# Transposing keys and queries of a head pair in two half-height tiles instead of one full-height tile

## The chip, the cores and the metric

The kernel runs on one core of a Trainium2 chip. A core has TensorE (PE; the loading of its stationary operand is shown apart, as PEld), VectorE (DVE), ScalarE (ACT), GpSimd (POOL) and SyncE (SP, which here issues nearly all DMAs). TensorE writes into PSUM, which has 8 banks of 512 fp32 columns on 128 partitions; VectorE and ScalarE read it from there. The metric is the device time of one execution in microseconds (us), as the median of several runs.

## What is computed

Everything is fp32. First comes attention with random features, for 8 batches of 8 heads, 576 tokens and head width 64; then a Fourier mix of its output with a two-layer network:

```python
def phi(x):                                  # q, k: (8, 8, 576, 64), scaled; omega: (128, 64)
    h = np.einsum('bhsd,md->bhsm', x, omega) - np.sum(x * x, -1, keepdims=True) / 2
    h = h - np.max(h, axis=-1, keepdims=True)
    return np.exp(h) / np.sqrt(m)
kv  = np.einsum('bhsm,bhsd->bhmd', phi(k), v);  z = np.sum(phi(k), axis=2)
x   = einsum('bhsm,bhmd->bhsd', phi(q), kv) / (einsum('bhsm,bhm->bhs', phi(q), z) + 1e-6)
u   = x + real(fft(fft(x, over tokens), over width))      # x as (8, 576, 512)
out = u + relu(normalised(u) @ w_ch1) @ w_ch2             # 512 -> 2048 -> 512
```

The subtraction of the maximum makes the term with the squares fall out, so the kernel computes only the projection, its maximum over the 128 features, and the exponential.

## The kernel before

**Two programs.** The work is written as streams: Python generators that yield a step (which engine or engines may do it, its assumed length, what it waits for, which buffers it takes and gives) and then issue that step's instructions. A planner (class `Listing`, from L100) runs at build time. It always picks the step that can begin first by its own clock, with small preferences (`bias`), and where a step may go to two engines it picks the one that would end first. Instructions go to each engine's queue in the order so picked, and each engine runs its queue in that order. It is a greedy order: nothing is searched, and no order is stored. The planner runs twice. The first program holds the attention, the Fourier mix, the conversion of the weights from another number format, and the preparation of the network; the second holds the network's matrix products.

**A pair.** The attention goes by pairs of heads, 4 per batch, 32 in all (`attn`, L580). Three streams run pairs side by side (`NS = 3`; stream i takes pairs i, i+3, ...). For each pair:

1. `loads` (L376) fetches keys and queries into one tile `kq` of 128 partitions and 18 x 64 columns, by two DMAs on SP's queue: the keys (event `("k", n)`), then the queries (event `("kq", n)`). There are two such tiles.
2. `transposed` (L502) turns the 9 chunks of 128 columns of `kq` into `kqT` by TensorE transposes (a matmul with the identity, L519). A chunk is 128 x 128, one transpose gives 128 columns. They come in groups of 4, 4 and 1; each group is a step, takes one PSUM bank, and is copied to SBUF by `evicted` (L523: ScalarE at L535 or VectorE at L533). The copy gives the bank back.
3. `pairs_of` (L599) projects on the features (matmuls at L613) in three steps of 4, 1 and 4 chunks. In the first six pairs the matmuls use two tiles of 64 rows x 128 columns of the TensorE array ("rows"), later four of 64 x 64 ("quarters"). Each step takes two adjacent PSUM banks ("duo").
4. `softmax` (L549): VectorE takes the maxima (L556), ScalarE the exponentials (L573, into tiles `e`). The exponentials of a bank give that bank back.
5. The products with the values (L647, quarters, a duo), the transposes of the queries' exponentials by the same helper `transposed` (groups of 1, 4 and 4, again at L519, tile `qeT`), and the numerator and denominator (L694 and L702, two tiles of 128 rows x 64 columns, "halves", a duo). VectorE divides (L711, L712, L723).

**Banks.** A step that takes a "bank" gets any one of the 8 that is free first, with a preference for one whose partner is in use. A step that takes a "duo" gets one of the 4 aligned pairs, once both of its banks are free (`banks_at`, L128).

**Tile shapes on TensorE.** Each step has a `mode`: "whole" (the default, and that of transposes), "rows", "halves" or "quarters". The planner adds 0.12 us where the mode changes between neighbouring steps.

The two places that the change rewrites, before:

```python
yield Step(PE, 0.109 * m, after=after(j0, j1), take=("bank",) + ..., give=give(j0, j1), bias=0.14)
...
for j in range(j0, j1):
    nc.tensor.transpose(ps[:, (j - j0) * 128 : (j - j0 + 1) * 128], src(j), ident[:])
yield Fork(evicted(dst, b, j0, j1, makes, order))
...
((0, 4), (4, 8), (8, R)),                      # groups of kqT, R = 9
lambda j0, j1: (("kq", n),) if j1 > 4 else (),  # the first group waits for the keys alone
```

Of the kernel before, what the change touches and what calls it, by code (L numbers as in the profile page):

```python
# [287 lines left out]
def kernel(  # L288
# [10 lines left out]
    nc = tc.nc  # L299

    B, H, S, D = q.shape
# [14 lines left out]
    R = S // 64  # L316
# [30 lines left out]
    ident = const.tile([128, 128], F32, name="ident")  # L347
# [11 lines left out]
        kq=NKQ, turned=NS, e=NE, e1=NS, kv=NS, x0=1, x1=1, fold=1, half=1, y=1,  # L359
# [3 lines left out]
    def psum_of(b):  # L363

        i = b.ids[0]
        return banks[:, i] if len(b.ids) == 1 else banks[:, i : i + 2]

    def got():

        return listing.got, psum_of(listing.got)  # L370
# [131 lines left out]
    def transposed(src, name, groups, after, makes, give, order=None):  # L502


        dst = None
        for j0, j1 in groups:
            m = j1 - j0
            yield Step(
                PE,
                0.109 * m,  # L510
                after=after(j0, j1),
                take=("bank",) + (("turned",) if j0 == 0 else ()),
                give=give(j0, j1), bias=0.14,
            )
            if dst is None:
                dst = att.tile([128, R, 128], F32, name=name, tag="turned")
            b, ps = got()
            for j in range(j0, j1):
                nc.tensor.transpose(ps[:, (j - j0) * 128 : (j - j0 + 1) * 128], src(j), ident[:])  # L519
            yield Fork(evicted(dst, b, j0, j1, makes, order))  # L520
        return dst

    def evicted(dst, b, j0, j1, makes, order):  # L523
        cost = (0.13 + 0.1 * (j1 - j0)) if order else 0.05 + 0.107 * (j1 - j0)
        step = Step(
            {ACT: cost, DVE: 0.06 + 0.133 * (j1 - j0) + (0.06 if order else 0.0)}, late=0.02,
            makes=makes + (j0,), give=(b,), bias=0.08,
        )
        yield step

        def copy(out, in_):
            if step.eng == DVE:
                nc.vector.tensor_copy(out=out, in_=in_)  # L533
            else:
                nc.scalar.activation(out=out, in_=in_, func=AF.Copy)  # L535

        ps = psum_of(b)[:, 0 : 128 * (j1 - j0)].rearrange("q (c p) -> q c p", p=128)
        dst = dst[:, j0:j1, :]
        if order is None:
            copy(dst, ps)  # L540
            return
        h, s, t = order[j0]
        dst = dst.rearrange("q c p -> q (c p)").rearrange("q (h s t c) -> q s h t c", h=h, s=s, t=t)
        ps = ps.rearrange("q c (h t s) -> q s h t c", h=h, s=s)
        for i in range(s):
            of = ps[:, i, :, ::-1, ::-1] if i and j0 else ps[:, i]
            copy(dst[:, i], of)
# [32 lines left out]
    def attn(n):  # L580
        b, pr = divmod(n, NP)

        yield Step(NONE, after=(("k", n),) + ((("vd", n - 1),) if n else ()))
        kq = kqs.pop(n)

        flat = kq[:].rearrange("p c d -> p (c d)")
        kqT = yield from transposed(
            lambda j: flat[:, 128 * j : 128 * j + 128],
            "kqT",
            ((0, 4), (4, 8), (8, R)),  # L590
            lambda j0, j1: (("kq", n),) if j1 > 4 else (),
            ("kqT", n),
            lambda j0, j1: ("kq",) if j1 == R else (),
        )
# [35 lines left out]
        def feature(c):  # L630
# [7 lines left out]
            mode="quarters",  # L638
            after=tuple(("e", n, t) for t in range(3)) + (("vd", n),),
            take=("duo",),  # L640
            give=("e", "e", f"vd{n % NV}"), bias=-0.19,
        )
        kvb, kvp = got()
        for r in range(R):
            for i, h in ((0, 0), (1, 1), (0, 1), (1, 0)):
                rows, cols = slice(D * i, D * i + D), slice(D * h, D * h + D)
# [9 lines left out]
        def keep():  # L656
# [8 lines left out]

        yield Fork(keep())
        qeT = yield from transposed(
            lambda j: feature(R + ORDER_R[j]),
            "qeT",
            ((0, 1), (1, 5), (5, R)),  # L670
            lambda j0, j1: tuple(
                ("e", n, t) for t in sorted({place(R + ORDER_R[j])[0] for j in range(j0, j1)})
            ),
# [7 lines left out]
            mode="halves",  # L681
            after=(("kv", n), ("qeT", n, 0), ("qeT", n, 1), ("qeT", n, 5)),
            take=("duo",),
            give=("turned", "kv"), bias=0.12,
# [28 lines left out]
        dst = x[:, :, 2 * D * pr : 2 * D * (pr + 1)].rearrange("p c (i d) -> p i c d", i=2)  # L713
# [281 lines left out]
    turned = {}  # L995
# [421 lines left out]
    def pairs(start):  # L1417
        for n in range(start, B * NP, NS):
            yield from attn(n)
# [770 lines left out]
```

## Time and profile before

| what | us |
|---|---|
| median of 3 runs (1218.25 to 1226.66) | 1223.65 |
| the profiled execution, its time | 1219.09 |
| its span, first to last instruction | 1217.3 |
| the first kq transpose starts | 4.4 |
| the last kq transpose starts | 356.6 |
| DVE busy in the first 92 us | 76.39 |
| PE busy in the 60 us from 380 to 440 us | 46.22 |
| PE busy in the 100 us from 440 to 540 us | 94.82 |

A profile is one execution taken by the hardware profiler. In a row such as `L519 PE MATMUL banks<-ident,kq 128*128 128x128 f32 x288 | 44.8, 296 | ...`, the parts are the line of the kernel, the engine, the operation, output and inputs, the stationary tile (rows*columns of the array), the moving operand (partitions x columns), the count, and then busy microseconds, mean nanoseconds of one, and the idle time of the engine just before, with what ended it. A matmul of fp32 is two instructions, a transpose is one. Matmuls overlap in the pipeline, so the length of one is its latency; what a matmul costs in a row of them is the distance from start to start. A busy share is an average over its window, and a wait counts only where it delays what ends last.

### The profile page before, as it was taken

The page shows a single profiled execution, that of the slowest core. Times are in us where ns is not written, and L with a number is a line of the kernel's source. Part 1 is how long each engine was busy: PE and PEld are TensorE (multiplying, and loading weights), DVE is VectorE, ACT ScalarE, POOL GpSimd, SP SyncE. Part 2 cuts the span into 40 slices and gives each one's busy share as a digit, 9 for nine tenths or more (in the row PEclk, how much of TensorE's full clock was granted, in tenths as well). Part 3 has the DMA queues.
Part 4 walks back from the last instruction along what each step waited for, and adds up shares of the span by engine and source line. Part 5 has one row for each costly group of instructions (what it writes and reads, how often), then busy time and mean ns, then how long its engine had stood idle before and what let it go on. Part 6 is the DMA issues. An engine that isn't in the chain of part 4 may idle for free.

```text
span 1217.3 us, 32303 instructions
## 1 busy us (share of the span) xinstructions
PE 1121.6 (92%) x12571; PEld 1034.9 (85%) x12571; DVE 974.1 (80%) x1788; ACT 582.1 (48%) x1795; POOL 276.5 (23%) x292
## 2 busy tenths in 40 slices
PE   8888987987579698999998999999999999999998
PEld 7776876876467588999998988999988999988998
DVE  6998999997878767777877687888867799757895
ACT  7867967967484183261253256322355222332221
POOL 2231332321010120032054125500036400044000
PEclk9998998998798799999999899999999999999999
DMA  9745845848743599898879877875776865757453
GB/s 250 228 143 152 246 119 173 244 136 267 235 162 101 155 312 288 259 288 276 271 224 272 280 245 204 263 202 157 236 210 202 262 183 176 211 150 225 134 156 110
DMA packets 209656, 255.83 MB, mean 210 GB/s; under 512 B 55264, under 2 KB 125152, under 8 KB 209504
## 3 DMA queue, kind: packets, MB, share of 16 engines
q1 hardware_dynamic: 209008, 253.50, 68.4%
q8 instruction: 100, 1.64, 0.6%
q14 instruction: 52, 0.43, 0.1%
q10 hardware_dynamic: 496, 0.26, 0.1%
HBM read 200.74 MB, written 57.15 MB: 212 GB/s over the span
## 4 chain that ended last, share of the span: by engine, by line
PE 76%; DVE 9%; ACT 8%; DMA 5%; issue 1%; SPq 0%; POOL 0%; DVEq 0%; ACTq 0%
PE banks L1954 31%; PE banks L1501 26%; ACT e L573 5%; PE banks L1658 4%; PE banks L613 4%; PE banks L647 3%; PE banks L519 3%; PE banks L694 2%; PE banks L806 2%; DVE nmx L556 2%; DMA wl<-w2l 2%; PE banks L816 1%; DMA raw<-in_moe_w_ch_dram 1%; DVE x L933 1%; ACT qeT L535 1%
## 5 line engine op out<-in xcount | busy, mean ns | idle before, releaser
L1954 PE MATMUL banks<-wl,sums 128*128 128x128 f32 x2016 | 250.4, 278 | 0.7 <-DMA wl<-w2l 0.5
L1954 PEld LDWEIGHTS banks<-wl,sums 128*128 128x128 f32 x2016 | 240.4, 195 | 1.6 <-issue 1.0
L573 ACT ACTIVATE e<-banks,nmx 128x128 f32<-128x128 f32 x576 | 159.3, 443 | 32.7 <-DVE nmx L556 32.7
L1954 PE MATMUL banks<-wl,hid 128*128 128x128 f32 x936 | 122.0, 278 | 8.7 <-DMA wl<-w2l 8.3
L1954 PEld LDWEIGHTS banks<-wl,hid 128*128 128x128 f32 x936 | 113.8, 194 | 9.9 <-issue 4.7
L613 PE MATMUL banks<-om,kqT 64*64 64x128 f32 (+1 forms) x2088 | 91.0, 295 | 29.9 <-ACT e L573 23.7
L613 PEld LDWEIGHTS banks<-om,kqT 64*64 64x64 f32 (+1 forms) x2088 | 75.7, 151 | 41.6 <-ACT e L573 29.3
L556 DVE TENSOR_REDUCE nmx<-banks 128x8 f32<-128x1024 f32 (+1 forms) x96 | 87.3, 951 | 20.4 <-PE banks L613 12.9
L1925 ACT ACTIVATE s<-banks 128x128 f32<-128x128 f32 x126 | 34.9, 277 | 132.9 <-PE banks L1954 116.4
L1501 PE MATMUL banks<-unw,wxw 128*128 128x256 f32 x352 | 85.5, 379 | 0.0
L1954 PE MATMUL banks<-wl,hx 128*128 128x128 f32 x576 | 74.3, 275 | 0.4 <-DVE part L1930 0.4
L1501 PEld LDWEIGHTS banks<-unw,wxw 128*128 128x128 f32 x352 | 66.5, 190 | 8.8
L1930 DVE TENSOR_TENSOR part<-banks,s 128x128 f32<-128x128 f32 x114 | 33.0, 290 | 49.6 <-PE banks L1954 44.4
L1501 PE MATMUL banks<-rx,wxw 128*128 128x256 f32 x288 | 71.1, 379 | 0.0
L1526 ACT ACTIVATE s<-banks 128x512 f32<-128x512 f32 x72 | 42.6, 595 | 57.9 <-PE banks L1501 52.2
L1501 PE MATMUL banks<-ttw,wxw 128*128 128x256 f32 x288 | 70.0, 379 | 0.0
L1954 PEld LDWEIGHTS banks<-wl,hx 128*128 128x128 f32 x576 | 69.4, 192 | 0.7 <-DVE part L1930 0.6
L462 POOL TENSOR_TENSOR w<-w,raw 128x512 f32<-128x512 f32 x30 | 41.4, 1379 | 124.9 <-DVE raw L456 110.3
L1501 PEld LDWEIGHTS banks<-rx,wxw 128*128 128x128 f32 x288 | 54.5, 190 | 7.3
L1501 PEld LDWEIGHTS banks<-ttw,wxw 128*128 128x128 f32 x288 | 54.5, 190 | 7.3
L519 PE MATMUL banks<-ident,kq 128*128 128x128 f32 x288 | 44.8, 296 | 17.0 <-ACT e L573 10.9
L1970 ACT ACTIVATE banks<-banks 128x128 f32<-128x128 f32 x63 | 16.6, 263 | 86.3 <-PE banks L1954 83.9
(244 smaller groups left out, 2398.0 us busy)
## 6 DMA issues: line engine op xcount, KB each, us to landing
wl<-w2l SPq DMA_DIRECT2D x294, 256.0 KB, 3.6
wxw<-w1x SPq DMA_DIRECT2D x120, 256.0 KB, 3.2
raw<-in_moe_w_ch_dram SPq DMA_DIRECT2D x32, 512.0 KB, 5.2
kq<-in_k_dram SPq DMA_DIRECT2D x32, 288.0 KB, 4.0
kq<-in_q_dram SPq DMA_DIRECT2D x32, 288.0 KB, 4.2
vd<-in_v_dram SPq DMA_DIRECT2D x32, 288.0 KB, 4.6
wx<-w1x SPq DMA_DIRECT2D x36, 256.0 KB, 3.3
u<-us SPq DMA_DIRECT2D x128, 64.0 KB, 3.1
```

Of the source, the lines that this page charges most:

```text
L462: eng.tensor_tensor(out=dst, in0=dst, in1=lof, op=ALU.add)
L519: nc.tensor.transpose(ps[:, (j - j0) * 128 : (j - j0 + 1) * 128], src(j), ident[:])
L556: nc.vector.tensor_reduce(nmx[:, :, 0:num], pps[:, :, 0 : MF * num].rearrange("p b (c m) -> p b c m", m=MF), axis=AX.X, op=ALU.max, negate ...
L573: nc.scalar.activation(out=e[:, c + (i if num == 1 else 0), :], in_=pps[:, i, MF * c : MF * c + MF], func=AF.Exp, bias=nmx[:, i, c : c + 1],)
L613: nc.tensor.matmul(pps[cols, c, MF * m : MF * m + MF], lhsT=kqT[rows, j, cols], rhs=om2[rows, :],)
L647: nc.tensor.matmul(kvp[cols, i, 0 : D + 1], lhsT=feature(r)[rows, cols], rhs=vds[n % NV][rows, r, :], start=(r == 0), stop=(r == R - 1),)
L1501: nc.tensor.matmul(ps[:, span * f : span * f + span].rearrange("f (b q) -> f b q", q=Q), lhsT=left[:, P * f : P * f + P], rhs=right, start ...
L1526: nc.scalar.activation(out=s[:], in_=ps, func=AF.Copy)
L1658: nc.tensor.matmul(cell.rearrange("f t (b q) -> f t b q", q=Q), lhsT=w[:, d, col : col + 128], rhs=right[:, :, d].rearrange("f (t b) q -> ...
L1925: nc.scalar.activation(out=s[:], in_=ps[:, 0:128], func=AF.Copy)
L1930: nc.vector.tensor_tensor(out=part[:, t, 128 * m : 128 * m + 128], in0=ps[:, 0:128], in1=saved[with_][:], op=ALU.add,)
L1954: nc.tensor.matmul(ps[:, 0:128], lhsT=left[:, f], rhs=wls[head(j), i, n][:, f], start=start and f == 0, stop=(f == 3), skip_group_check=True,)
```

## The change

The first 8 of a pair's 9 key and query transposes become one step. It takes a duo instead of two single banks, waits for keys and queries, and issues two transposes per chunk: rows 0 to 63 of the chunk into the duo's first bank, rows 64 to 127 into its second, 64 columns each, in two tiles of 64 rows ("rows"). The step's assumed length is 0.07 us per chunk instead of 0.109. The two copies of 4 chunks each follow one after the other in one stream; each reads 64 columns per chunk from both banks, and the second one gives both banks back. The ninth chunk stays a whole transpose into a single bank. The transposes of the exponentials (`qeT`) keep their groups and their form. The order is again the planner's greedy one, made anew from the changed steps.

```diff
-        for j0, j1 in groups:
+        for parts in groups:
+            j0, j1 = parts[0][0], parts[-1][1]
             m = j1 - j0
+            split = len(parts) > 1
             yield Step(
                 PE,
-                0.109 * m,
+                (0.07 if split else 0.109) * m,
+                mode="rows" if split else "whole",
                 after=after(j0, j1),
-                take=("bank",) + (("turned",) if j0 == 0 else ()),
+                take=("duo" if split else "bank",) + (("turned",) if j0 == 0 else ()),
                 give=give(j0, j1), bias=0.14,
             )
...
             for j in range(j0, j1):
+                if split:
+                    for r in range(2):
+                        rows = slice(D * r, D * r + D)
+                        nc.tensor.transpose(
+                            ps[:, r, (j - j0) * D : (j - j0 + 1) * D], src(j)[rows, :], ident[rows, rows]
+                        )
+                    continue
                 nc.tensor.transpose(ps[:, (j - j0) * 128 : (j - j0 + 1) * 128], src(j), ident[:])
-            yield Fork(evicted(dst, b, j0, j1, makes, order))
+            yield Fork(evicted(dst, b, parts, makes, order))
...
-    def evicted(dst, b, j0, j1, makes, order):
+    def evicted(dst, b, parts, makes, order):
+        for j0, j1 in parts:
+            yield from copied(dst, b, j0, j1, parts, makes, order)
+
+    def copied(dst, b, j0, j1, parts, makes, order):
+        split = len(parts) > 1
...
-            makes=makes + (j0,), give=(b,), bias=0.08,
+            makes=makes + (j0,), give=(b,) if j1 == parts[-1][1] else (), bias=0.08,
...
+        dst = dst[:, j0:j1, :]
+        if split:
+            k0 = D * (j0 - parts[0][0])
+            ps = psum_of(b)[:, :, k0 : k0 + D * (j1 - j0)].rearrange("q r (c p) -> q c r p", p=D)
+            copy(dst.rearrange("q c (r p) -> q c r p", r=2), ps)
+            return
...
-            ((0, 4), (4, 8), (8, R)),
-            lambda j0, j1: (("kq", n),) if j1 > 4 else (),
+            (((0, 4), (4, 8)), ((8, R),)),
+            lambda j0, j1: (("kq", n),),
...
-            ((0, 1), (1, 5), (5, R)),
+            (((0, 1),), ((1, 5),), ((5, R),)),
```

More of the change, by code (lines that the diff above doesn't have):

```diff
@@ L535, in copy @@
                 nc.scalar.activation(out=out, in_=in_, func=AF.Copy)
+        dst = dst[:, j0:j1, :]
[4 more added lines that the diff above has]
+            return
         ps = psum_of(b)[:, 0 : 128 * (j1 - j0)].rearrange("q (c p) -> q c p", p=128)
-        dst = dst[:, j0:j1, :]
         if order is None:
```

## The prediction

> **What bounds it now.** I read the page first (busy times, then the chain that ended last), then the busy time by stretches, then the order of TensorE's work around the transposes, then the rows of the tiles kq and kqT and the waits. From the page:
>
> ```profile
> PE 1121.6 (92%) x12571; PEld 1034.9 (85%) x12571; DVE 974.1 (80%) x1788; ACT 582.1 (48%) x1795; POOL 276.5 (23%) x292
> ...
> L519 PE MATMUL banks<-ident,kq 128*128 128x128 f32 x288 | 44.8, 296 | 17.0 <-ACT e L573 10.9
> ```
>
> TensorE at 92% is an average over two programs. The transposes of keys and queries (288 = 32 pairs x 9) all lie in the first of them: the last starts at 356.6 us. The busy times by stretches split it (columns: window, length, then PE, PEld, DVE, ACT, POOL with instruction counts, granted clock, DMA share, GB/s):
>
> ```profile
> 92.00:184.00 92.00, 77.99 (x1760) 66.95 (x1760) 84.98 (x163) 72.34 (x272) 27.97 (x21) 0.93 0.60 175
> 184.00:276.00 92.00, 77.34 (x1760) 66.62 (x1760) 86.06 (x167) 73.72 (x283) 25.58 (x21) 0.94 0.62 184
> 276.00:380.00 104.00, 79.90 (x1654) 68.36 (x1654) 79.48 (x158) 69.17 (x259) 12.93 (x12) 0.87 0.63 207
> ...
> 540.00:1217.00 677.00, 667.24 (x4837) 635.31 (x4835) 527.14 (x930) 229.33 (x573) 157.05 (x175) 0.99 0.70 213
> ```
>
> From 540 us on TensorE is the bound (99%), and the change does not touch that work. In the attention stage VectorE is the fullest: 85 to 86 us of 92 (93%), TensorE 84 to 85%, ScalarE 79 to 80%. The same 1,760 matmuls come back in each 92 us: the order repeats every 8 pairs. So TensorE time saved here is worth only what it takes out of waits.
>
> **The step itself.** TensorE's order, first where projections in row tiles stand beside kq transposes, then around another pair (start, length, work, count):
>
> ```profile
> 27.48 1.28 PE L647 MATMUL banks<-vd,e 64*64 64x65 f32 x72
> ...
> 31.94 0.40 PE L702 MATMUL banks<-kv,qeT 128*64 128x65 f32 x8
> 32.27 2.28 PE L613 MATMUL banks<-om,kqT 64*128 64x128 f32 x36
> 34.48 1.09 PE L519 MATMUL banks<-ident,kq 128*128 128x128 f32 x8
> ```
>
> ```profile
> 136.55 1.28 PE L647 MATMUL banks<-vd,e 64*64 64x65 f32 x72
> 137.76 0.33 PE L519 MATMUL banks<-ident,e 128*128 128x128 f32 x1
> 137.93 1.15 PE L519 MATMUL banks<-ident,kq 128*128 128x128 f32 x9
> ...
> 140.28 2.20 PE L613 MATMUL banks<-om,kqT 64*64 64x128 f32 x72
> 142.40 1.15 PE L694 MATMUL banks<-kv,qeT 128*64 128x65 f32 x32
> ```
>
> A group's length is its count of steps plus one matmul's latency (0.27 us for 128 columns, 0.23 for 65). Removed: whole transposes cost (1.15-0.27)/8 = 0.110 us each, so 8 cost 0.88. Added: 16 half-height ones, 8 rounds of two row tiles with 64 moving columns. No row has that shape. The nearest by moving length are the 65-column rounds: quarters (1.28-0.23)/71 x 4 = 0.059 us, halves (1.15-0.23)/31 x 2 = 0.059. The nearest by tile (64x128, two row tiles) is (2.28-0.27)/35 x 2 = 0.115, but with 128 columns moving. So a round costs 0.059 to 0.115. I take 0.059, because the moving length sets the step in all three. The other candidate is the weight load, still 128 columns wide:
>
> ```profile
> L613 PEld LDWEIGHTS banks<-om,kqT 64*128 64x128 f32 x216 | 13.5, 188 | 2.0 <-ACT kqT L535 0.9 <-ACT e L573 0.5 <-issue 0.2
> L519 PEld LDWEIGHTS banks<-ident,kq 128*128 128x128 f32 x288 | 34.7, 150 | 23.1 <-ACT e L573 14.6 <-DVE x L723 5.7 <-ACT kqT L535 0.9
> ...
> L694 PEld LDWEIGHTS banks<-kv,qeT 128*64 128x64 f32 x1024 | 34.2, 140 | 10.8 <-DVE bmp L925 4.3 <-issue 2.0 <-ACT qeT L535 2.0
> ```
>
> A transpose's load (150 ns, mean) is nearer to a 64-column load (140), which keeps a 0.059 round, than to a 128-column load of a matmul (188). I lean on that. The Trainium skill, "TensorE: Matmul & The Clock Gate", section on LDWEIGHTS, says otherwise: a load's time goes by its columns, about columns/1.2 ns, whatever the rows, so halving the height saves nothing; for 128 columns that is an estimate of 107 ns per round, and the saving below would be 0.8 us in place of 13.1. The load rows by line contradict it for transposes as far as a length can.
>
> Saved: 8 x (0.110-0.059) = 0.41 us per pair, 13.1 us over 32 pairs (by the upper end a loss of 8 x 0.005 x 32 = 1.3).
>
> **Changes of tile shape.** Between groups of different tile shape a gap shows: the last of the eight L702 starts at 31.94+0.40-0.23 = 32.11, the next group at 32.27, 0.16 us later where a round takes 0.06: 0.10 us. After L613 it is 142.40-(140.28+2.20-0.27) = 0.19 against 0.09 to the next round: 0.10 again. Eight half-height ones, then the ninth whole: one change more where quarters or halves stand on both sides, two more where a whole transpose went before (as at 137.76), none between row-tile projections (34.48, in the first six pairs). Taken as 1.5 x 32 x 0.10 = 4.8 us, ends 0 and 6.4. Net TensorE time: 13.1-4.8 = 8.3 us saved, 0.26 per pair.
>
> **What of it reaches the end.** In 92 to 276 us VectorE's idle time before its maxima (L556) that a projection (L613) ended is 5.5 us in 6 waits. A kq step 0.26 us shorter shortens each by at most that: 6 x 0.26 = 1.6 us in 184 us, 3.3 over the 380 us of the stage. The rest of the 8.3 us becomes TensorE idle time behind VectorE. Taken: -3.3, ends 0 and -13.1.
>
> **Evictions.** 64 copies of 512 columns (ScalarE 655 ns each) stay; each now reads both banks in runs of 64. The row of that kind, ScalarE's copy into y (L829: 256 columns over two banks in runs of 64), takes 429 ns; between the 362 of 128 columns and the 655 of 512, a straight line gives 460. So no surcharge (ends -30 and +30 ns, 2 us of ScalarE time either way, beside its 20% idle). But both banks are held until the second copy is done, and the first copy is placed only after all 8 transposes.
>
> **The wait for two banks.** The step now asks for an adjacent pair. In the repeating order TensorE has one long wait, at the kq transposes, for exponentials that free banks:
>
> ```profile
> 185.58 2.28 ACT L573 ACTIVATE e<-banks,nmx 128x128 f32<-128x128 f32 x8 [4.39 <-DVE nmx L556]
> 186.78 0.66 PE L519 MATMUL banks<-ident,kq 128*128 128x128 f32 x4 [4.07 <-ACT e L573]
> 187.73 0.62 ACT L535 ACTIVATE kqT<-banks 128x512 f32<-128x512 f32 x1
> 187.91 1.33 PE L519 MATMUL banks<-ident,kq 128*128 128x128 f32 x5 [0.48 <-ACT e L573]
> 188.21 1.17 ACT L573 ACTIVATE e<-banks,nmx 128x128 f32<-128x128 f32 x4
> ```
>
> The first four start on one bank at 186.78, the rest on the next at 187.91. Needing both, all wait until 187.91, with the projections (L613) queued behind them, and the first copy (0.62 us at 187.73) moves behind. I charge that copy, 0.65 us, once per period, 4 periods: +2.6 us.
>
> **The load.** The first step now waits for the queries too, the second DMA of the pair, issued 0.4 us after the keys on SP's queue. Later pairs' loads are issued some 6 us before use (180.05, used 186.78) and land in 4.2: covered. If that lead is gone, 0.6 us per pair. The first pair is exposed: +0.5 us once.
>
> **Sum.** -3.3+2.6+0.5 = -0.2 us: 1218.9 against the profiled execution's 1219.09 (span 1217.3 and 1.8 around it). That execution lies 4.6 us under the median 1223.65, so in the median's terms 1223.4, rounded to 1223.
>
> **Rivals.** (1) Slower by bank waits: each time a transpose waits for exponentials (12.5 us, 11 times in the first 460 us), the second bank comes one set of four exponentials later (1.17 us at 188.21), and the projections behind do not catch up: 11 x 1.17 = 12.9, 1236. It decides from about three such waits on, where it eats the 3.3. For: the waits are there at single banks; against: at 190.63 the projection waited for the later copy anyway. Also the Trainium skill's "TensorEngine Tiling (Array Packing)", section on restrictions, warns that row tiling raises pressure on PSUM banks; the rows above show the banks already short.
> (2) The loads set the round, or the halves run in turn, so that the change does not do what it says: no saving, 4.8+1.3 us of extra TensorE time of which a third to all arrives, plus 3.1: +5 to +9, 1229 to 1233. For: the row-tile row at 0.115; against: the short transpose load.
> (3) Faster: TensorE is most of the chain of waits also in this stage, and all of 8.3 to 13.1 lands: 1210 to 1215. Against: VectorE at 93%.
> (4) The list order falls into another cycle: the 4.3 us hole per period goes or comes twice, 4 times: 1206 or 1241.
>
> **Chances.** Forecast (1217 to 1230) 0.48; (1) 0.20; (2) 0.10; (3) 0.14; (4) 0.08, half each way. A measurement tells 1% (12.2 us) from no change. Slower by more: half of (1), half of (4), and tails of the forecast and (2), 0.06: 0.20. Faster: a third of (3), half of (4) and 0.02 of tail: 0.11. Within: 0.69. The range takes in (3), (2), (1) and the near part of (4): 1208 to 1239.
>
> **What would show it.** In the changed profile: 512 half-height transposes (64x64 moving) at 0.059 us a round, against 0.115 for (2); gaps of 0.10 at more shape changes; the period still near 92 us with VectorE at 93%; idle time before L519 by exponentials about as now, and near 24 us in all for (1). The prediction is wrong if the period changes by over 3 us, or if VectorE's share drops while TensorE's idle time grows.

## The result and the profile after

The changed kernel takes 1233.34 us (median of 6 runs, 1229.96 to 1236.46), the kernel before, run beside it, 1221.56 (6 runs, 1218.25 to 1226.66). The ratio is 1.0091, with a 95% interval of 1.0071 to 1.0110: slower by 0.9% (11 us by the ratio, 12 by the medians), where no change was forecast. The profiled execution spans 1228.2 us, against 1217.3.

First the busy times of the changed kernel's page, then its busy times by stretches, with the windows and columns of before:

```profile
PE 1120.8 (91%) x12827; PEld 1035.4 (84%) x12827; DVE 972.0 (79%) x1777; ACT 574.9 (47%) x1752; POOL 279.4 (23%) x310
```

```profile
92.00:184.00 92.00, 75.25 (x1779) 66.15 (x1768) 82.92 (x154) 69.61 (x254) 30.07 (x25) 0.89 0.61 182
184.00:276.00 92.00, 75.22 (x1775) 65.17 (x1775) 84.24 (x158) 68.23 (x256) 26.14 (x24) 0.93 0.66 194
276.00:380.00 104.00, 79.76 (x1699) 67.88 (x1699) 83.37 (x161) 66.96 (x249) 15.66 (x20) 0.87 0.59 196
380.00:440.00 60.00, 42.68 (x357) 33.79 (x356) 36.06 (x80) 12.87 (x47) 8.12 (x7) 0.72 0.34 105
...
540.00:1217.00 677.00, 670.12 (x4866) 638.68 (x4866) 530.91 (x933) 234.07 (x583) 162.94 (x184) 0.99 0.71 214
```

The stretch from 380 to 440 us of the kernel before:

```profile
380.00:440.00 60.00, 46.22 (x253) 38.01 (x252) 45.38 (x95) 20.18 (x56) 9.11 (x11) 0.86 0.58 189
```

From 540 us on TensorE is as full as before (99%). From 92 to 276 us TensorE, VectorE and ScalarE are all emptier: VectorE has 82.92 and 84.24 of 92 us (84.98 and 86.06 before), TensorE 75 (77 to 78 before). The emptiest stretch is 380 to 440 us, where VectorE had 45.38 us of work before and has 36.06 now, at a granted clock of 0.72 (before 0.86).

Next, the rows of the changed step, by shape, up to 400 us:

```profile
L525 PE MATMUL banks<-ident,kq 64*128 64x64 f32 x512 | 25.2, 242 | 7.7 <-ACT e L593 5.8 <-DVE bmp L933 0.9 <-DVE x L743 0.5
L525 PEld LDWEIGHTS banks<-ident,kq 64*128 64x128 f32 x512 | 21.0, 150 | 11.9 <-ACT e L593 6.4 <-issue 2.0 <-DVE x L743 1.2
...
L550 ACT ACTIVATE kqT<-banks 128x512 f32<-128x512 f32 x63 | 35.2, 613 | 25.8 <-PE banks L525 25.7
L529 PE MATMUL banks<-ident,kq 128*128 128x128 f32 x32 | 9.4, 329 | 3.5 <-DVE x L743 2.6 <-ACT e L593 1.0
```

TensorE's idle time before these transposes has fallen, from 17.0 to 7.7+3.5 = 11.2 us. ScalarE's idle time before the copies into kqT, waiting for the transposes, has risen to 25.8. The same row of before, by shape:

```profile
L535 ACT ACTIVATE kqT<-banks 128x512 f32<-128x512 f32 x57 | 33.9, 655 | 4.2 <-PE banks L519 3.9
```

The two waits of over 4 us for exponentials before kq transposes that the kernel before has in its repeating part, at 94.4 and 186.8 us, are gone. But TensorE now waits about as long in other places. From the waits of the changed kernel (what waited, for what, us in all, times, longest):

```profile
PE banks L633 <- DVE bmp L945: 8.1, 2, 4.1
PE banks L1119 <- ACT e L593: 5.1, 2, 4.7
```

These are projections (L633) that wait for the Fourier mix on VectorE, and transposes of the network's preparation (L1119) that wait for exponentials.

**Where the 11 us appear.** The last steps of the first program, from the timelines of the two traces:

| step | before | after | later by |
|---|---|---|---|
| the last pair's kq transposes start | 355.1 | 365.7 | 10.6 |
| the last maximum starts | 366.5 | 373.3 | 6.8 |
| the last division starts | 378.7 | 401.6 | 22.9 |
| the last folds of the Fourier mix start | 395.4 | 410.3 | 14.9 |
| the first sum after the mix that waits for a DMA (rx) starts | 415.1 | 428.7 | 13.6 |
| the first product of the second program (wl) starts | 448.0 | 460.8 | 12.8 |
| from there to the end of the span | 769.3 | 767.4 | -1.9 |

So in these two executions all of it lies ahead of the second program. In the changed kernel's order of TensorE's work, one line stands out (start, length, work, count, idle time before and what ended it):

```profile
357.78 0.71 PE L525 MATMUL banks<-ident,kq 64*128 64x64 f32 x16
358.42 0.33 PE L529 MATMUL banks<-ident,kq 128*128 128x128 f32 x1
...
375.72 3.62 PE L1678 MATMUL banks<-unT,w 128*128 128x256 f32 x16
...
385.84 8.90 PE L1678 MATMUL banks<-unT,w 128*128 128x256 f32 x40
...
395.58 1.15 PE L714 MATMUL banks<-kv,qeT 128*64 128x65 f32 x32
...
399.90 1.31 PE L714 MATMUL banks<-kv,qeT 128*64 128x65 f32 x30 [0.22 <-ACT qeT L550]
...
406.60 2.50 PE L826 MATMUL banks<-cs_sb,fold 128*128 128x160 f32 x8 [5.16 <-DVE fold L799]
```

The network's first products (L1678) run before the last two pairs' numerators (L714), which VectorE and then the last batch's mix (L826) wait for. In the kernel before the same three kinds of work stand the other way round:

```profile
375.53 1.65 PE L694 MATMUL banks<-kv,qeT 128*64 128x65 f32 x32
377.25 1.10 PE L694 MATMUL banks<-kv,qeT 128*64 128x65 f32 x32
...
382.44 3.72 PE L1658 MATMUL banks<-unT,w 128*128 128x256 f32 x16
```

### The profile page after: what moved, and what is told of

Its sections match the earlier page's. It is cut to its first block, busy times and chain, and to the rows that moved or that the text cites. A ratio compares the mean times of both kernels' runs of the same rounds, so it can differ in the third digit from the quotient of the medians.

```text
span 1228.2 us, 32758 instructions
## 1 busy us (share of the span) xinstructions
PE 1120.8 (91%) x12827; PEld 1035.4 (84%) x12827; DVE 972.0 (79%) x1777; ACT 574.9 (47%) x1752; POOL 279.4 (23%) x310
## 4 chain that ended last, share of the span: by engine, by line
PE 61%; DMA 2%; DVE 2%; ACT 0%; SPq 0%; issue 0%; POOL 0%; DVEq 0%
PE banks L1974 31%; PE banks L1521 27%; PE banks L1678 2%; DMA wl<-w2l 2%; DMA w1x<-rx 0%; DVE ttw L1318 0%; DVE so L1477 0%; DVE w1s L1424 0%; DMA wxw<-w1x 0%; DVE unxw L1215 0%; DVE rx L1477 0%; DMA us<-x 0%; SPq L967 0%; DVE unw L1215 0%; DVE hid L1564 0%
## 5 line engine op out<-in xcount | busy, mean ns | idle before, releaser
L633 PE MATMUL banks<-om,kqT 64*64 64x128 f32 (+1 forms) x2088 | 96.5, 308 | 36.8 <-ACT e L593 22.7
L633 PEld LDWEIGHTS banks<-om,kqT 64*64 64x64 f32 (+1 forms) x2088 | 81.8, 161 | 47.3 <-ACT e L593 26.9
L667 PE MATMUL banks<-vd,e 64*64 64x65 f32 x2304 | 52.1, 245 | 4.8 <-ACT kqT L550 1.9
```

The costliest lines, as they stand in the source:

```text
L633: nc.tensor.matmul(pps[cols, c, MF * m : MF * m + MF], lhsT=kqT[rows, j, cols], rhs=om2[rows, :],)
L667: nc.tensor.matmul(kvp[cols, i, 0 : D + 1], lhsT=feature(r)[rows, cols], rhs=vds[n % NV][rows, r, :], start=(r == 0), stop=(r == R - 1),)
```

## The experiments

The change does several things at once: another form of transposes, a common pair of banks, a common wait, and through the planner another order of the whole first program. The planner sees a step's assumed length, its mode, its buffers and its waits, but not the instructions it issues. So an order can be kept while the instructions are exchanged, and the other way round. Four explanations were tried: the new order alone, with its tail part (the products ahead of the last numerators); the new form; the clock of TensorE, which a shorter step may let fall; and the first copy, which now waits for more. Ratios below are to the kernel before, run beside each; where two changed kernels are compared, their ratios are, because the kernel before had slightly different medians (1221.56 to 1223.80).

### The form at a fixed order

e1: the changed kernel's order, but whole transposes, four in each bank, and copies that read one bank.

```diff
                 if split:
-                    for r in range(2):
-                        rows = slice(D * r, D * r + D)
-                        nc.tensor.transpose(
-                            ps[:, r, (j - j0) * D : (j - j0 + 1) * D], src(j)[rows, :], ident[rows, rows]
-                        )
+                    r, c = divmod(j - j0, 4)
+                    nc.tensor.transpose(ps[:, r, 128 * c : 128 * c + 128], src(j), ident[:])
                     continue
...
-            k0 = D * (j0 - parts[0][0])
-            ps = psum_of(b)[:, :, k0 : k0 + D * (j1 - j0)].rearrange("q r (c p) -> q c r p", p=D)
-            copy(dst.rearrange("q c (r p) -> q c r p", r=2), ps)
+            ps = psum_of(b)[:, (j0 - parts[0][0]) // 4].rearrange("q (c p) -> q c p", p=128)
+            copy(dst, ps)
```

> The changed kernel with its order kept instruction for instruction (the planner is given the same numbers), but the 8 transposes of the pair of banks are whole ones, 4 in each bank, and each copy reads its own bank. Theory ORDER (the half-height transposes do save TensorE time; the loss comes from the order that the greedy planner makes out of the new step): at the same order the whole ones cost 8 x (0.110-0.061) = 0.39 us per pair and save about 0.1 us of shape change, 9 us of TensorE time in all, of which a quarter to all arrives: 1235.5 to 1242 against 1233.3 of the changed kernel. Theory TILE (the half-height form itself costs the time, by shape changes and waits): equal or faster than the changed kernel, down to the 1221.6 of before.

Measured: 1228.04, ratio 1.0035 (1.0011 to 1.0059). The half-height form at this order gives 1.0091: it costs 0.56%, and the intervals don't meet. That is 6.8 us by the ratios, 5.3 by the medians. The changed order with the old form is still slower than before, by 0.35% or 4.3 us. The rows of e1 that stand against those of the changed kernel above:

```profile
L547 ACT ACTIVATE kqT<-banks 128x512 f32<-128x512 f32 x63 | 36.2, 618 | 23.1 <-PE banks L524 21.2 <-DVE rden L727 0.6 <-DVE x L739 0.6
```

With the old form, too, ScalarE is idle for 23.1 us before these copies (25.8 in the changed kernel, 4.2 before). So nearly all of that wait came with the order. The two profiled executions took 1229.51 (e1) and 1229.96 us, closer together than the medians: in them the first wl product starts 5.7 us later with the half-height form, but the time from there to the end is 5.2 us shorter. So the loss at the end is a matter of the medians, not of these two traces.

e2: the kernel before with the common step and the common wait alone. Transposes whole, the planner told 0.109 us per chunk and the mode "whole". So it has an order of its own.

```diff
-                take=("bank",) + (("turned",) if j0 == 0 else ()),
+                take=("duo" if split else "bank",) + (("turned",) if j0 == 0 else ()),
...
-            ((0, 4), (4, 8), (8, R)),
-            lambda j0, j1: (("kq", n),) if j1 > 4 else (),
+            (((0, 4), (4, 8)), ((8, R),)),
+            lambda j0, j1: (("kq", n),),
```

> The kernel before with one part of the change: the 8 transposes stay whole, but are one step with a pair of banks, held until the second copy, waiting for keys and queries; the planner is given their true cost (0.109 us each, mode whole). Theory BANK (asking for two banks at once costs the time): slower than before by most of the 11.8 us, 1229 or more, with more TensorE idle time ahead of the kq transposes than the 17.0 us of before. Theory ORDER: nothing systematic; a new order, somewhere within 10 us of 1221.6 on either side.

Measured: 1217.57, ratio 0.9960 (0.9937 to 0.9983). Two banks at once and one wait for both loads cost nothing in an order that the planner makes for them.

e3: e2's order, with the half-height transposes and copies of the change put in (the first edit, turned round).

```diff
-                    r, c = divmod(j - j0, 4)
-                    nc.tensor.transpose(ps[:, r, 128 * c : 128 * c + 128], src(j), ident[:])
+                    for r in range(2):
+                        rows = slice(D * r, D * r + D)
+                        nc.tensor.transpose(
+                            ps[:, r, (j - j0) * D : (j - j0 + 1) * D], src(j)[rows, :], ident[rows, rows]
+                        )
...
```

> The same order as e2 (the planner is given 0.109 us and mode whole), but the 8 transposes are issued half-height, 64 rows to a bank. Theory ORDER: faster than e2 by a quarter to all of 8 us of TensorE time, 2 to 8 us. Theory TILE: equal to e2 or slower.

Measured: 1220.42, ratio 0.9980 (0.9960 to 1.0001), against e2's 0.9960: no gain again, and a loss of 0.2% that the overlapping intervals don't settle.

### The tail of the order

e4: the changed kernel, its first products held until the last two pairs are divided.

```diff
     def first_products():
-        yield Step(NONE, after=("w2 done",))
+        yield Step(NONE, after=("w2 done", ("x", B - 1, NP - 2), ("x", B - 1, NP - 1)))
```

> The changed kernel, but the first products of the network (L1678 there), which in it stand ahead of the last two pairs' numerators on TensorE from 375.7 us on, wait for the last two pairs' outputs. Theory ORDER, tail part: the last pair's division comes near 380 instead of 401.8 us, and of the 11.8 us of loss 5 to 10 go: 1223 to 1228. Rival: the products only move behind and are waited for there, so that the time stays at 1231 to 1236, and the loss lies in the steady part (a period of 95 instead of 92 us).

Measured: 1230.08, ratio 1.0060 (1.0040 to 1.0080). The same stretch of TensorE's order in e4:

```profile
385.89 1.31 PE L714 MATMUL banks<-kv,qeT 128*64 128x65 f32 x30 [0.22 <-ACT qeT L550]
...
390.39 14.08 PE L1678 MATMUL banks<-unT,w 128*128 128x256 f32 x64
...
410.87 2.50 PE L826 MATMUL banks<-cs_sb,fold 128*128 128x160 f32 x8 [5.49 <-DVE fold L799]
```

The last division starts at 387.5, 14 us earlier than after the change. But now the products (14.08 us) stand ahead of the mix, which starts at 410.87 and not at 406.60; the first wl product starts at 460.7, as after the change at 460.8. So the striking line of the timeline is worth 0.3% of the 0.9% at most (the intervals overlap), and nothing by this trace. The order paid for it in the next place.

### The clock and the first copy

At one place of the same order, e1 and the changed kernel part by 2.6 us. TensorE's order in e1, then in the changed kernel:

```profile
187.71 1.09 PE L524 MATMUL banks<-ident,kq 128*128 128x128 f32 x8 [1.47 <-ACT e L589]
...
190.20 1.28 PE L663 MATMUL banks<-vd,e 64*64 64x65 f32 x72 [1.29 <-ACT kqT L547]
191.30 2.15 PE L629 MATMUL banks<-om,kqT 64*64 64x128 f32 x72
193.38 1.09 PE L524 MATMUL banks<-ident,kq 128*128 128x128 f32 x8
```

```profile
189.10 0.96 PE L525 MATMUL banks<-ident,kq 64*128 64x64 f32 x16 [1.47 <-ACT e L593]
...
191.59 2.23 PE L667 MATMUL banks<-vd,e 64*64 64x65 f32 x72 [1.26 <-ACT kqT L550]
193.59 3.89 PE L633 MATMUL banks<-om,kqT 64*64 64x128 f32 x72
197.41 0.71 PE L525 MATMUL banks<-ident,kq 64*128 64x64 f32 x16
```

The same 144 matmuls take 3.2 us in e1 (190.20 to 193.38) and 5.8 in the changed kernel (191.59 to 197.41). The busy times of the changed kernel in stretches of 3.4 us show TensorE at half its clock there (the columns as above; the last but two is the granted clock):

```profile
183.50:186.90 3.40, 3.40 (x82) 2.99 (x85) 3.26 (x8) 2.20 (x9) 2.15 (x4) 1.00 0.62 212
186.90:190.30 3.40, 1.93 (x43) 1.33 (x35) 3.40 (x4) 2.65 (x10) 3.40 (x5) 1.00 0.59 155
190.30:193.70 3.40, 2.14 (x77) 2.12 (x80) 3.37 (x12) 2.70 (x9) 1.38 (x3) 0.51 0.85 246
193.70:197.10 3.40, 3.40 (x73) 3.40 (x72) 3.13 (x6) 1.31 (x5) 0.30 (x1) 0.50 0.74 205
```

After a stretch in which TensorE was busy for 1.93 of 3.40 us the granted clock is 0.5 for two stretches. In e1 the same place has the same busy time, and the clock stays up:

```profile
185.50:188.90 3.40, 1.94 (x35) 1.47 (x27) 3.40 (x4) 2.64 (x10) 3.40 (x5) 1.00 0.65 168
188.90:192.30 3.40, 2.11 (x112) 2.10 (x115) 3.37 (x12) 3.35 (x13) 1.38 (x3) 1.00 0.88 262
```

So the busy time alone doesn't tell when the clock falls; the last section has an estimate that does better. The other difference is the first copy into kqT. One pair in the changed kernel, then one in e1:

```profile
197.41 0.71 PE L525 MATMUL banks<-ident,kq 64*128 64x64 f32 x16
198.16 1.08 ACT L550 ACTIVATE kqT<-banks 128x512 f32<-128x512 f32 x2 [2.97 <-PE banks L525]
```

```profile
193.38 1.09 PE L524 MATMUL banks<-ident,kq 128*128 128x128 f32 x8
194.07 1.08 ACT L547 ACTIVATE kqT<-banks 128x512 f32<-128x512 f32 x2 [1.21 <-PE banks L524]
```

The sixteen half-height transposes take 0.71 us, the eight whole ones 1.09. But the copy starts 0.75 us after the first half-height transpose and 0.69 after the first whole one: it reads both banks, so it waits for all sixteen; a copy of one bank needs only the first four. Over all 32 pairs of the two traces, taken pair by pair, the first copy comes later after its first transpose by 0.06 us in the median and 0.15 in the mean. In both timelines above TensorE's next work waited for such a copy (the lines that an ACT kqT ended). Four runs tried to part the clock from the copy.

e5: the changed kernel, each half-height transpose issued twice, so that TensorE works longer and a clock that fell for want of work would stay up.

```diff
-                    for r in range(2):
+                    for r in (0, 1) * 2:
```

> The changed kernel, its order kept, but each of the 16 half-height transposes is issued twice into the same place (32 in all), 0.49 us more TensorE time per pair, 15.6 us over 32 pairs. Theory CLOCK (the shorter step leaves more stretches of 3.4 us in which TensorE is busy less than 0.4 of the time; after such a stretch its clock is granted at half, and the half-speed stretches cost more than the step saved): with the time put back there are fewer half-speed stretches, near e1's 79 us in the first 430 us instead of the changed kernel's 102, and the time falls to e1's, 1226 to 1230, although TensorE does more. Rival TILE (the half-height form costs by its shape changes, which are here unchanged): no gain, and the added work makes it slower by a quarter to all of 15.6 us: 1237 to 1249.

Measured: 1241.74, ratio 1.0142 (1.0115 to 1.0168), 0.51% or 6.2 us above the changed kernel. Eight rounds of 0.065 us (worked out below) in 32 pairs are 16.6 us of added TensorE time, so about a third arrives. The half-speed time ahead of the second program went from 102 us to 92 only (e1: 79), each in one profiled execution; the expectation's 102 and 79 are these, while the first 430 us alone have 93 and 75, and 73 in this run. Over whole spans, the mean granted clock of the six runs is 0.953 to 0.961, against 0.949 to 0.955 in the changed kernel and 0.957 to 0.967 in e1's runs. So the clock did rise, and the time did not fall. But the added work also delays the first copy, so this run alone doesn't decide.

e6: e2 with each whole transpose issued twice.

```diff
-                    nc.tensor.transpose(ps[:, r, 128 * c : 128 * c + 128], src(j), ident[:])
+                    for _ in range(2):
+                        nc.tensor.transpose(ps[:, r, 128 * c : 128 * c + 128], src(j), ident[:])
```

> e2 (whole transposes, a pair of banks, its own order) with each of the 8 whole transposes issued twice, 0.88 us more TensorE time per pair, 28 us over 32 pairs. Theory CLOCK says that work in this place can pay for itself where it lifts a stretch over 0.4, but e2 already has few half-speed stretches (72 us in the first 430): between e2's 1217.6 less 4 and plus 8, fewer half-speed stretches than e2. Rival TILE: slower than e2 by a quarter to all of 28 us, 1225 to 1245.

Measured: 1240.38, ratio 1.0131 (1.0103 to 1.0159), against e2's 0.9960: +1.71% or 20.9 us, for 8 x 0.110 x 32 = 28.2 us of added work ahead of the copies. So time in this step is far from free: three quarters of it arrive. That suggests, without showing it, that a saving which brought the copies forward would count.

e9: e1 with chunk j in bank j mod 2, so that the first copy must wait for all eight whole transposes; the work of TensorE and the order are e1's.

```diff
-                    r, c = divmod(j - j0, 4)
+                    c, r = divmod(j - j0, 2)
                     nc.tensor.transpose(ps[:, r, 128 * c : 128 * c + 128], src(j), ident[:])
...
-            ps = psum_of(b)[:, (j0 - parts[0][0]) // 4].rearrange("q (c p) -> q c p", p=128)
-            copy(dst, ps)
+            c0 = (j0 - parts[0][0]) // 2
+            ps = psum_of(b)[:, :, 128 * c0 : 128 * c0 + 256].rearrange("q r (c p) -> q c r p", p=128)
+            copy(dst.rearrange("q (c r) p -> q c r p", r=2), ps)
```

> e1 (the changed kernel's order, 8 whole transposes), but chunk j goes to bank j modulo 2 of the pair, so that the first copy reads both banks and must wait for all 8 transposes, as the changed kernel's first copy must for all 16. TensorE's work and the order are those of e1; only the first copy starts later, by about 0.4 us where ScalarE waits for it. Theory COPY (what the pair waits for is the first copy, which in e1 starts 0.69 us after the first transpose and in the changed kernel 0.75: the half-height step saves nothing there): slower than e1, 3 to 12 us, 1231 to 1240. Rival: TensorE's time is what counts, and the time stays at e1's, 1226 to 1230.

Measured: 1232.06, ratio 1.0077 (1.0044 to 1.0110), 0.42% above e1's 1.0035. The intervals overlap (up to 1.0059 and from 1.0044), so it supports a cost of the later first copy without proving its size. And this copy is much later than the changed kernel's: by 0.44 us in the median pair against e1 (mean 0.45), where the half-height form makes 0.06 (mean 0.15). In proportion to the measured 0.42%, an estimate, the later copy would account for 0.06% to 0.14% of the 0.56% that the half-height form loses to e1, about a quarter at most. The rest would need another cause.

e10: the changed kernel, the ninth transpose issued four times. This adds work behind the common step and leaves the first copies alone.

```diff
-                nc.tensor.transpose(ps[:, (j - j0) * 128 : (j - j0 + 1) * 128], src(j), ident[:])
+                for _ in range(4 if name == "kqT" else 1):
+                    nc.tensor.transpose(ps[:, (j - j0) * 128 : (j - j0 + 1) * 128], src(j), ident[:])
```

> The changed kernel, its order kept, with the ninth transpose, which is whole and stands behind the 16 half-height ones in a bank of its own, issued four times: 0.33 us of TensorE time per pair, about what the half-height form saved, put back behind the two copies that the projections wait for. Theory CLOCK: fewer half-speed stretches, and the time falls towards e1's, 1226 to 1230. Rival (clock of no weight, TensorE's time counts in part): slower by a quarter to all of 10.5 us, 1236 to 1244.

Measured: 1235.66, ratio 1.0106 (1.0064 to 1.0147): 0.15% above the changed kernel, within the intervals. So 3 x 0.110 x 32 = 10.6 us of TensorE time behind the copies cost little or nothing, but they don't win back what e1 has over the changed kernel either. The mean clock of the first 430 us is the last column but two (the changed kernel, e1, e10):

```profile
0.00:430.00 430.00, 342.77 (x7179) 294.66 (x7179) 349.77 (x672) 287.95 (x1048) 104.82 (x106) 0.89 0.59 178
```

```profile
0.00:430.00 430.00, 344.37 (x6926) 296.09 (x6927) 355.24 (x682) 289.29 (x1048) 105.08 (x106) 0.91 0.60 182
```

```profile
0.00:430.00 430.00, 351.84 (x7273) 302.92 (x7274) 347.83 (x669) 289.45 (x1047) 104.56 (x106) 0.90 0.58 176
```

These are single executions. Over the whole span of every run the clock of e10 is 0.954 to 0.962 (mean 0.959), the changed kernel's 0.949 to 0.955 (mean 0.953). So in e5 and e10 the added work brought the clock part of the way back, and in neither did the time fall to e1's 1226 to 1230, as the clock theory had forecast. That the added 10.6 us of e10 cost so little may be the clock's doing. Two things are seen: half-speed stretches lie where e1 and the changed kernel part, and the clocks of their runs (0.957 to 0.967 and 0.949 to 0.955) don't overlap. That the lower clock is the cause of the loss isn't shown: in the rows above the clock fell after a stretch with waits, so it may be a consequence of them.

### The order

An order here includes the choice of engine, where the planner has one. TensorE's instructions are the same in the changed kernel, e8 and e11 (12,827); of the other engines' steps a few change place (ScalarE has 1,752, 1,751 and 1,765).

e7: the kernel before with one line of the diff, so that the first group waits for the queries too. No instruction is edited.

```diff
             ((0, 4), (4, 8), (8, R)),
-            lambda j0, j1: (("kq", n),) if j1 > 4 else (),
+            lambda j0, j1: (("kq", n),),
```

> The kernel before with one line of the change: the first group of transposes waits for the queries too, not for the keys alone. Groups of 4, 4 and 1 whole transposes in single banks as before. Theory ORDER: the wait itself is covered (loads lead by some 6 us), but the planner makes another order of it, and the time lands anywhere within 15 us of 1221.6, on either side. Rival WAIT (the later start is what costs): slower by 2 to 10 us.

Measured: 1206.87, ratio 0.9864 (0.9840 to 0.9889). A wait added, and the kernel is 1.4% faster.

e8: the changed kernel's instructions; the planner is told the mode "whole" for the common step, and so doesn't charge the change of shape.

```diff
                 (0.07 if split else 0.109) * m,
-                mode="rows" if split else "whole",
+                mode="whole" if split else "whole",
```

> The changed kernel with the same instructions, but the planner is told that the half-height step needs no change of tile shape (mode whole instead of rows, 0.07 us each kept). Nothing but the order differs. Theory ORDER: the time moves by 3 to 15 us from 1233.3 on either side, more likely down, since the changed kernel's order has the last two pairs behind the network's products. Theory TILE: the time stays within 3 us of 1233.3, since every cost of the step is still there.

Measured: 1217.07, ratio 0.9939 (0.9920 to 0.9959), 1.5% faster than the changed kernel, with the same work in another order.

e11: as e8, and the planner is told 0.075 us per chunk in place of 0.07. Of some 70 such changes of the planner's numbers, this is the one whose order ends soonest by its own clock.

```diff
-                (0.07 if split else 0.109) * m,
-                mode="rows" if split else "whole",
+                (0.075 if split else 0.109) * m,
+                mode="whole" if split else "whole",
```

> The changed kernel with the same instructions, but the planner is given 0.075 us per chunk instead of 0.07 and mode whole instead of rows; of some 70 such small changes of numbers this order closes soonest by the planner's own clock. Theory ORDER: as fast as e7, 1200 to 1212, so that the spread over orders of the same instructions is over 20 us. Rival TILE: not below 1217.

Measured: 1203.33, ratio 0.9849 (0.9810 to 0.9888), the fastest version found, 30 us under the changed kernel.

e12: e11's order with e1's whole transposes and copies.

```diff
-                    for r in range(2):
-                        rows = slice(D * r, D * r + D)
-                        nc.tensor.transpose(
-                            ps[:, r, (j - j0) * D : (j - j0 + 1) * D], src(j)[rows, :], ident[rows, rows]
-                        )
+                    r, c = divmod(j - j0, 4)
+                    nc.tensor.transpose(ps[:, r, 128 * c : 128 * c + 128], src(j), ident[:])
...
```

> The order of e11, kept, with 8 whole transposes in place of the 16 half-height ones, 4 in each bank. The third comparison of the two forms at one order, after e1 against the changed kernel (whole faster by 0.56%) and e2 against e3 (whole faster by 0.2%). Theory COPY: equal or faster than e11, by 0 to 7 us. If half-height is worth its TensorE time: slower than e11 by 3 to 9 us.

Measured: 1203.95, ratio 0.9856 (0.9815 to 0.9897). At the best order, too, the form makes no difference that can be told.

The first products with wl, in the rows of the changed kernel, e7 and e11 (count, shortest, median and longest in ns, first and last start in us):

```profile
L1974 PE MATMUL banks<-wl,hid x936: 272/275/423, 460.8 to 1214.6; 128*128 128x128 f32 x188
```

```profile
L1954 PE MATMUL banks<-wl,hid x936: 272/275/426, 432.6 to 1189.8; 128*128 128x128 f32 x188
```

```profile
L1974 PE MATMUL banks<-wl,hid x936: 272/275/426, 432.7 to 1188.4; 128*128 128x128 f32 x188
```

The second program starts 28 us earlier in e7 and e11. And the stretch from 380 to 440 us of e11, to be held against the row shown for the changed kernel:

```profile
380.00:440.00 60.00, 56.68 (x277) 48.19 (x278) 41.91 (x79) 29.03 (x64) 9.79 (x12) 0.89 0.70 237
```

TensorE is busy 56.68 of 60 us there, against 42.68: the network's preparation is already running. All orders side by side, ordered by time (from the timelines; the order of instructions is the same within a block):

| kernel | last pair's kq transposes | last division | first wl product | median | ratio |
|---|---|---|---|---|---|
| e11 half-height | 347.2 | 363.2 | 432.7 | 1203.33 | 0.985 |
| e12 whole | 346.7 | 362.8 | 433.6 | 1203.95 | 0.986 |
| | | | | | |
| e7 | 351.9 | 365.9 | 432.6 | 1206.87 | 0.986 |
| | | | | | |
| e8 half-height | 356.4 | 375.1 | 447.4 | 1217.07 | 0.994 |
| | | | | | |
| e2 whole | 355.9 | 378.6 | 446.1 | 1217.57 | 0.996 |
| e3 half-height | 359.1 | 381.7 | 448.5 | 1220.42 | 0.998 |
| | | | | | |
| before | 355.1 | 378.7 | 448.0 | 1221.56 | 1 |
| | | | | | |
| e1 whole | 359.6 | 395.7 | 455.1 | 1228.04 | 1.004 |
| changed, half-height | 365.7 | 401.6 | 460.8 | 1233.34 | 1.009 |

From the first wl product to the end of the span all of them take 766 to 773 us. Between the blocks the time moves by up to 30 us; within them by 5.3 at most.

## Why the prediction was wrong

It forecast no change (1223) and got +0.9%; 1233 lies in the range given, outside the forecast's own 1217 to 1230.

**The steps that failed** are two. The first is the frame of the sum: it took the period of 92 us with its waits as it stood and added -3.3, +2.6 and +0.5 to it. The greedy order did not stand. After the change the pairs 0, 8, 16 and 24 start at 4.7, 88.9, 177.9 and 278.5 us: the third period takes 100.6, where before (176.3 to 268.5) it took 92.2. Most of that comes with the order alone: 97.1 in e1. Both of the text's signs for a wrong prediction are met, a period changed by over 3 us, and VectorE's share falling while TensorE's idle time grows. The second is the term of -3.3, as follows below. Of the 0.91%, the new order makes 0.35% (e1 with the old form) and the form 0.56% (the changed kernel against e1).

Rival (4), another cycle of the order, is nearest to what happened, with a chance of 0.08 and its two ends at 1206 and 1241. Its price, a wait of some 4 us before the transposes that goes or comes twice, is not what was seen: that wait went, others of its size came elsewhere, and the time rose. The same work gave 1203, 1217 and 1233 in three orders, a spread of more than the whole loss. A changed order deserved most of the chance, and both signs about alike.

**The round: right.** The last of sixteen starts at 0.71 less the latency of one, 0.22, so 15 steps are 0.49 us and a round of two is 0.065; forecast 0.059, bounds 0.059 to 0.115. That refutes rival (2). In the Trainium skill, "TensorE: Matmul & The Clock Gate", the section on LDWEIGHTS has a load take its columns over 1.2 in ns, whatever the rows, from which the estimate for a round is 107 ns; the trace has 65, and the measurement decides.

**The gap between shapes: right where looked at.** The last half-height transpose starts at 357.78+0.49 = 358.27, the ninth at 358.42: 0.15 where a round takes 0.065, so 0.09; forecast 0.10. How many such gaps were added wasn't counted.

**What reaches the end (-3.3): wrong.** At fixed orders the form costs 0.56% (the changed kernel against e1), 0.2% (e3 against e2) and -0.07% (e11 against e12), none of them a gain beyond its interval. The prediction asked how much TensorE time is saved, and then let a part of it shorten VectorE's waits. What the next step waits for is the copy, and the first copy starts no earlier (0.75 us against 0.69). That the copy of four chunks would now wait for all eight is in the prediction, but under the evictions and with no price. This is why there is no gain; it is too small for the loss of 0.56% in the changed kernel's order, by the proportion to e9 about a quarter of it.

**Evictions: right.** At the same order the half-height copies take 613 ns and the whole ones, from one bank each, 618 (e1); in e3 and e2 both take 650. So there is no surcharge for reading two banks.

**The wait for two banks (+2.6) and rival (1): not borne out.** Idle time before the transposes fell from 17.0 to 11.2 us, and e2, which takes both banks at once, is faster than before, though in an order of its own. The new wait sits on ScalarE instead, 25.8 us before the copies, and e1's 23.1 puts it down to the order.

**The load (+0.5):** the first transposes start at 4.7 us instead of 4.4, so 0.3. In e7 the same wait is worth -1.4%, by the order that comes of it.

**Rival (3),** all of the saving landing, was seen nowhere: 1203 us needs e11's order, and the old form has it there too.

What stays open: why the form costs 0.56% in the changed kernel's order and nothing in e11's. The later copy and half-speed stretches are both in the trace of the first, and the runs here don't share the loss out between them.

## What to carry to other kernels

Where a planner makes the order greedily at build time, test an edit of a step's form at a fixed order (by telling the planner the same numbers) and then over several orders, before anything is credited to the edit: here the order moved the time by 2.4%, the form by 0.6% at most. A shorter step brings little if what the next engine waits for comes no earlier; look at the start of the first copy, not only at the busy time of the engine. And a line that looks wrong in the timeline may be worth little, as in e4, because the work moved past it is late somewhere else.

## What the runs showed of the hardware

**The clock followed TensorE's load over some 3.4 us.** In the 14 traces the granted clock is 1.00 or 0.50, for stretches of 3.41 us or a multiple of it. The busy time doesn't separate the stretches (1.93 and 1.94 us of 3.40, above). An estimate does better: each matmul is charged 0.110 us per 128 moving columns, divided by the number of tiles side by side, and the charges in a stretch are summed (over the first 1190 us). The 206 stretches before a fall to half then have at most 0.39 of their time charged, and the 4,291 full-speed stretches that another one followed at least 0.34. With twice the charge at half speed, the clock came back after stretches of 0.70 or more and stayed at half after up to 0.84. So the edges lie within these bounds, as far as such an estimate goes. The Trainium skill, "TensorE: Matmul & The Clock Gate", Part 1 on the clock gate, speaks of an idle stretch of about 3.4 us; here a stretch with 1.93 of 3.40 us busy was enough. Ahead of the second program, 58 us (e12) to 102 us (the changed kernel, e10) of a profiled execution ran at half speed; 72 before.

**A row-tiled pair of outputs ties two banks together.** Halving the transposes shortens the group from 0.82 us (first start to last) to 0.49, and yet delays the first copy by 0.06, because each copy needs a part of both banks. With whole transposes spread over both banks (e9) the first copy starts at least 1.06 us after the first transpose; with four in each bank (e1), from 0.58 us on.
